# Late stages of a local-attention and feed-forward kernel: probabilities scaled in place in float32, split into two halves by one copy and one subtraction per two heads, with another table of scheduling numbers

## The chip, the cores and the metric

The kernel runs on one core of a Trainium2 chip. The metric is the device time of one execution in microseconds (us). The core has five engines that run side by side, each through a queue of its own in a fixed order: TensorE (PE, matrix products; PEld is its weight load), VectorE (DVE), ScalarE (ACT), GpSimd (POOL) and SyncE (SP, which here only issues DMAs). An engine that waits holds back everything behind it in its queue.

## The reference

For 4 batches of 768 positions with 8 heads of 64, every query sees the keys less than 16 positions away, and 24 block keys (the maxima of blocks of 32 keys, whose values are the blocks' means). The result of all heads, 3072 rows of 512, goes through two matrices with a SiLU between them.

```python
k_sum = k.reshape(B, H, nb, block, D).max(axis=3)
v_sum = v.reshape(B, H, nb, block, D).mean(axis=3)
scores_l = scale * np.matmul(q, k.transpose(0, 1, 3, 2))
...
scores_s = scale * np.einsum('bhsd,bhnd->bhsn', q, k_sum)
scores_s = scores_s + np.log(block)
...
a = np.exp(scores_all)
a = a / (np.sum(a, axis=-1, keepdims=True) + 1e-09)
...
h = x @ w_in
g = h * (1.0 / (1.0 + np.exp(-h)))
return (g @ w_out).astype(np.float32)
```

## The kernel before

**Tiles.** Attention runs over 24 tiles of 128 queries (s = 0 to 23, six for each batch b). Each query half of 64 sees 120 keys (64 + 32 local ones and 24 block keys), so that a head's scores are 128 x 120. The feed-forward part runs over 12 chunks of 256 rows (c = 0 to 11, two tiles each), and each chunk over 16 slices f of the 2048 inner columns.

**Number formats.** Attention of batch 0 and the whole of chunk 0 are computed in float32. From batch 1 on (the late stages of the title), queries, keys, probabilities and values are each split into a float16 part and the float16 rest of it, and a product is the sum of three float16 products. From chunk 1 on the feed-forward products are made in the same way, with weights that are split on the chip once their largest magnitude is known.

**One feed-forward step** (job_f): 12 matmuls of 256 columns into a bank (L818, float32: L815 and L837), tanh on ACT (L842), its product with the bank on DVE (L843), the float16 part on ACT (L845), the rest on DVE (L846), and 6 matmuls of 512 columns (L826, float32: L823) that add to two output banks. After the 16th step the output banks are scaled into a staging buffer (L871 on ACT, L872 on DVE) and written out (L873).

**One late attention tile:** scores on PE (job_scores, L591, 48 matmuls), then in job_a for each pair of heads: mask and row minimum of the negated scores on DVE (L627), exponential and row sum on ACT (L630), the inverse sums on DVE (L635, L636), the scaled probabilities in float16 (L670 by the helper `scaled`, on DVE, ACT or POOL: L645, L641, L643), and the rest of them, `e * sum - p`, on DVE (L674, two instructions per two heads). A DMA transposes the 128 x 512 tile of two heads and both parts (L677). Then 48 matmuls with the values (job_c, L709) and a copy with its split into x (job_x, L725 and L726). The values come by DMA, are scaled (L560, L561), copied to float16 (helper `copy`: L231 ACT, L233 POOL, L235 DVE) and their rest is taken (helper `less`: L238, on POOL or DVE). In tiles of batch 0 PE transposes the probabilities (L656) and multiplies them (L694).

**The weights:** 16 slices are loaded (L737), put right bit by bit (L755 and L751 on ACT, L753 and L757 on DVE), and their largest magnitude is taken (L758 on DVE). When all are there, a chain finds one scale: DVE L776, PE L781, DVE L785 to L790, PE L794, DVE L795 (it writes `ws`). Only then can the slices be split (L771 ACT or L772 DVE for the first part, L773 DVE for the rest), and L818 of chunk 1 can begin.

**Banks.** The score banks of all tiles from s = 4 on are 6 and 3 (L576); bank 3 is also an output bank of chunk 0, so its first scores wait until L871 has emptied it. Staging buffers for loads, outputs and values are a ring of three (`raw`).

**What sets the order.** All steps are handed to a planner (class Plan) with a cost for each engine that could do them, the keys that they read and write, and a priority. A sweep over a model of the machine picks the engine and the order; several rounds with priorities from a backward sweep follow. DVE and POOL steps that touch the port they share are never put side by side (`port`). Where PE would idle in the first stage, the planner puts filling matmuls (L325). The priorities come from the table TUNE, so that a change of a cost or of that table moves steps on all engines. Within an engine the order is then fixed in the program.

Of the kernel before, what the change touches and what calls it, by code (L numbers as in the profile page):

```python
# [16 lines left out]
ALU = mybir.AluOpType  # L17
# [5 lines left out]
P = 128  # L23
# [7 lines left out]
NKEY = HALF + BLK + NB  # L31
# [193 lines left out]
def local_attn_ffn(ctx: ExitStack, tc: tile.TileContext, qkT, qP, qF, kF, v, vR, vP, w, out):  # L225
# [383 lines left out]
    def job_a(m, prio):  # L609
# [28 lines left out]
        def scaled(e, out, j, i):  # L638
            by, src = su4[:, 2 * j + i:2 * j + i + 1], e_t[ns[j]][:, i, :]
            if e == "act":  # L640
                nc.scalar.activation(out=out, in_=src, func=AF.Copy, scale=by)  # L641
            elif e == "pool":
                nc.gpsimd.tensor_scalar(out=out, in0=src, scalar1=by, scalar2=0.0, op0=ALU.mult, op1=ALU.add)  # L643
            else:
                nc.vector.tensor_scalar(out=out, in0=src, scalar1=by, scalar2=None, op0=ALU.mult)  # L645
# [19 lines left out]
        for j, n in enumerate(ns):  # L665
            pk, et = (m + j) % NP, e_t[n]
            pt, (tt, ttk) = p_t[pk], tt_of(m + j)
            pkeys = [("p", pk, i) for i in range(2)]
            for i in range(2):
                plan.op({"dve": 235, "act": 296, "pool": 320}, lambda e, i=i, j=j, pt=pt: scaled(e, pt[:, i, :NKEY], j, i), r=[sum_key(j, i), ("e", n, i)], w=[pkeys[i]], prio=prio)  # L670

            def low(e, pt=pt, et=et, j=j):
                for i in range(2):
                    nc.vector.scalar_tensor_tensor(out=pt[:, i, P:P + NKEY], in0=et[:, i, :], scalar=su4[:, 2 * j + i:2 * j + i + 1], in1=pt[:, i, :NKEY], op0=ALU.mult, op1=ALU.subtract)  # L674

            plan.op({"dve": 510}, low, r=[sum_key(j, i) for i in range(2)] + [("e", n, i) for i in range(2)], w=pkeys, prio=prio)
            plan.op({"dma": 1250}, lambda e, tt=tt, pt=pt: nc.sync.dma_start_transpose(out=tt, in_=pt.rearrange("p a b -> p (a b)")), r=pkeys + ["third"], w=[ttk], prio=prio)  # L677

    def job_c(m, prio):
# [277 lines left out]
    plan.issue()  # L957


TUNE = dict(vd=145.25, ws=-1296.0, s0=-1306.0, wp=-955.25, wm=1695.25, km=296.75, w_dma=-551.75, w_dec=-1473.75, a0=-15.0, a1=-399.75, d1=7.75, span=34.25, post=1219.25, ffn2=350.75, jc0=150.5, jc1=208.75, jx0=-166.75, jx1=-108.0, vs=25.0, qk=66.0, k=57.5, v=2313.0, v0=-101.0, out=-36.75, first=771.75)  # L960


NUDGE = {}
# [58 lines left out]
```

## Time and profile before

| what | value |
|---|---|
| three timed runs, median (lowest to highest) | 599.84 us (599.81 to 600.15) |
| the profiled execution: its own time | 599.46 us |
| its span (first to last instruction) | 597.8 us |
| first matmul, last matmul start | 1.4 us, 593.8 us |
| ACT, share of the span | 62% |
| granted TensorE clock over the span | 1.00 |
| moved by DMA | 75.29 MB |

The span is what the views of the trace divide; 1.7 us of the execution lie outside it. In a timeline row stand the start and the length in us, the engine, the line, the operation, the tiles (out<-in), how many instructions were merged, and in brackets the idle time before it with what ended it. PE's rows are longer than its pace, since matmuls overlap; float32 matmuls appear as two instructions each.

### The profile page before, as it was taken

What the parts mean: (1) busy time and instruction counts of PE and PEld (TensorE: products, weight loads), DVE (VectorE), ACT (ScalarE), POOL (GpSimd) and SP (SyncE); (2) the same over time, 40 slices, a digit from 0 to 9 for tenths busy, and PEclk for the clock granted to TensorE, in tenths of its full rate; (3) what the DMA queues carried; (4) which work ended last, traced back from release to release, by engine and by line L of the source; (5) the groups of instructions that cost most, each with busy time, mean ns of one, the idle gap of its engine ahead of it and who ended that gap; (6) DMA issues with size and microseconds to landing.
All of it is one profiled execution on the core that took longest, in us unless ns stands there. A gap on an engine that the chain in (4) does not pass through costs nothing.

```text
span 597.8 us, 15304 instructions
## 1 busy us (share of the span) xinstructions
PE 588.6 (98%) x5848; PEld 399.7 (67%) x5848; DVE 440.1 (74%) x1338; ACT 372.2 (62%) x1014; POOL 108.6 (18%) x164
## 2 busy tenths in 40 slices
PE   8999999999999999999999999999999999999997
PEld 5666656676666666666666666666766766666664
DVE  6999979997886748979896555979898764333332
ACT  4998859777757756647675544756777554333332
POOL 3211201035421000043330020014241400000000
PEclk9999999999999999999999999999999999999999
DMA  8999532135765634543646530442734401000001
GB/s 334 410 420 412 174 123 98 27 87 152 153 128 172 157 90 128 90 133 97 123 129 174 166 89 36 120 122 62 169 93 106 111 2 36 36 1 2 35 1 37
DMA packets 60916, 75.29 MB, mean 126 GB/s; under 512 B 41914, under 2 KB 42170, under 8 KB 59050
## 3 DMA queue, kind: packets, MB, share of 16 engines
q1 hardware_dynamic: 60842, 74.31, 41.9%
q8 instruction: 46, 0.75, 0.5%
q14 instruction: 28, 0.23, 0.1%
HBM read 56.79 MB, written 6.29 MB: 106 GB/s over the span
## 4 chain that ended last, share of the span: by engine, by line
PE 82%; DVE 9%; DMA 4%; ACT 3%; issue 1%; SPq 1%; DVEq 0%; ACTq 0%
PE bank L826 37%; PE bank L818 37%; PE bank L709 3%; DVE wm L758 2%; PE bank L591 2%; DVE wr L757 2%; DMA raw<-in_qkT_dram 1%; DMA second<-in_qP_dram 1%; DVE e L627 1%; PE bank L694 1%; ACT wr L771 1%; PE bank L656 1%; DVE t L843 1%; PE bank L837 1%; DMA raw<-in_qF_dram 1%
## 5 line engine op out<-in xcount | busy, mean ns | idle before, releaser
L818 PE MATMUL bank<-x,wr 128*128 128x256 f16 x2112 | 258.1, 273 | 0.0
L818 PEld LDWEIGHTS <-wr 128*128 128x128 f16 x2112 | 205.6, 98 | 57.2 <-issue 0.6
L826 PE MATMUL bank<-wr,gh 128*128 128x512 f16 x702 | 209.1, 380 | 0.4 <-ACT gh L845 0.4
L843 DVE SCALAR_TENSOR_TENSOR t<-t,bank 128x256 f32<-128x256 f32 x192 | 80.1, 417 | 85.9 <-ACT t L842 85.0
L842 ACT ACTIVATE t<-bank,th 128x256 f32<-128x256 f32 x176 | 82.1, 467 | 92.7 <-PE bank L818 92.4
L826 PE MATMUL bank<-wr,gl 128*128 128x512 f16 x351 | 133.1, 379 | 0.1
L845 ACT ACTIVATE gh<-t 128x256 f16<-128x256 f32 x176 | 72.9, 414 | 72.3 <-DVE t L843 69.4
L846 DVE SCALAR_TENSOR_TENSOR gl<-t,gh 128x256 f16<-128x256 f32 x176 | 86.6, 493 | 40.4 <-ACT gh L845 40.0
L826 PEld LDWEIGHTS <-gh 128*128 128x128 f16 x702 | 65.9, 98 | 44.6 <-ACT gh L845 0.7
L630 ACT ACTIVATE e<-e,mx 128x120 f32<-128x120 f32 x192 | 73.2, 383 | 12.9 <-DVE mx L627 12.7
L826 PEld LDWEIGHTS <-gl 128*128 128x128 f16 x351 | 34.3, 98 | 43.7 <-DVE gl L846 3.0
L674 DVE SCALAR_TENSOR_TENSOR first<-e,sum,first 128x120 f16<-128x120 f32 x144 | 49.8, 394 | 0.3 <-POOL first L643 0.3
L643 POOL TENSOR_SCALAR first<-e,sum 128x120 f16<-128x120 f32 x52 | 22.0, 433 | 125.7 <-ACT gh L845 39.6
L627 DVE CUSTOM_DVE_ANT_0 e<-bank,masks,qsc 128x120 f32<-128x120 f32 x144 | 42.2, 336 | 2.8 <-PE bank L591 2.8
L630 ACT ACTIVATION_READ_ACCUMULATOR e<-e,mx 128x1 f32 x192 | 36.4, 190 | 0.0
L238 POOL TENSOR_TENSOR first<-raw,first 120x1024 f16<-120x1024 f32 x14 | 30.4, 2173 | 10.9 <-ACT first L231 5.4
L823 PE MATMUL bank<-wr,t 128*128 128x512 f32 x64 | 30.7, 599 | 0.0
L815 PE MATMUL bank<-x,wr 128*128 128x256 f32 x112 | 26.3, 379 | 0.0
L815 PEld LDWEIGHTS bank<-x,wr 128*128 128x128 f32 x112 | 21.0, 190 | 7.0 <-issue 4.1
L643 POOL TENSOR_SCALAR e<-e,sum 128x120 f32<-128x120 f32 x28 | 11.2, 412 | 71.4 <-DVE sum L636 61.8
L561 POOL TENSOR_SCALAR raw<-raw,vsc 120x1024 f32<-120x1024 f32 x10 | 11.7, 1167 | 55.5 <-PE bank L818 31.0
L773 DVE SCALAR_TENSOR_TENSOR wr<-wr,ws 128x1024 f16<-128x1024 f32 x16 | 20.2, 1274 | 0.1
(146 smaller groups left out, 598.1 us busy)
## 6 DMA issues: line engine op xcount, KB each, us to landing
wr<-in_w_dram SPq DMA_DIRECT2D x14, 1024.0 KB
raw<-in_qkT_dram SPq DMA_DIRECT2D x18, 576.0 KB
out_dram<-raw SPq DMA_DIRECT2D x23, 256.0 KB
raw<-in_kF_dram SPq DMA_DIRECT2D x12, 384.0 KB
raw<-in_qF_dram SPq DMA_DIRECT2D x9, 512.0 KB
raw<-in_vR_dram SPq DMA_DIRECT2D x12, 384.0 KB
raw<-in_v_dram SPq DMA_DIRECT2D x18, 208.0 KB
raw<-in_v_dram SPq DMA_DIRECT2D x18, 192.0 KB
```

What stands on the lines that cost most here:

```text
L627: plan.op({"dve": 262 if b else 206}, lambda e, i=i, j=j, et=et, mx=mx: nc.vector.tensor_tensor_reduce(out=et[:, i, :], in0=sc[j][:, i, :N ...
L630: plan.op({"act": 385}, lambda e, i=i, j=j, et=et, mx=mx: nc.scalar.activation(out=et[:, i, :], in_=et[:, i, :], func=AF.Exp, scale=-1.0, ...
L643: nc.gpsimd.tensor_scalar(out=out, in0=src, scalar1=by, scalar2=0.0, op0=ALU.mult, op1=ALU.add)
L674: nc.vector.scalar_tensor_tensor(out=pt[:, i, P:P + NKEY], in0=et[:, i, :], scalar=su4[:, 2 * j + i:2 * j + i + 1], in1=pt[:, i, :NKEY], o ...
L815: nc.tensor.matmul(out=h, lhsT=wi[:, ct * P:(ct + 1) * P], rhs=x0[:, ct, :], start=(ct == 0), stop=(ct == NCT - 1))
L818: nc.tensor.matmul(out=h, lhsT=wip[:, part, ct * P:(ct + 1) * P], rhs=x[:, ct, :], start=(ct == 0 and q == 0), stop=(ct == NCT - 1 and q = ...
L823: nc.tensor.matmul(out=bank[ob[u]], lhsT=t[:, u * P:u * P + P], rhs=wo, start=opens, stop=closes)
L826: nc.tensor.matmul(out=bank[ob[u]], lhsT=g[:, u * P:u * P + P], rhs=wop[:, part, :], start=(opens and q == 0), stop=(closes and q == 2))
L842: plan.op({"act": 264 if c == 0 else 360}, lambda e: nc.scalar.activation(out=t, in_=h, func=AF.Tanh, scale=0.5 if c == 0 else th[:, 0:1]) ...
L843: plan.op({"dve": 337}, lambda e: nc.vector.scalar_tensor_tensor(out=t, in0=t, scalar=1.0, in1=h, op0=ALU.add, op1=ALU.mult), r=bk(k), w=[ ...
L845: plan.op({"act": 311}, lambda e: nc.scalar.activation(out=gh, in_=t, func=AF.Copy, scale=SHRINK), r=[("t", j)], w=[("gh", n)], prio=post)
L846: plan.op({"dve": 343}, lambda e: nc.vector.scalar_tensor_tensor(out=gl, in0=t, scalar=SHRINK, in1=gh, op0=ALU.mult, op1=ALU.subtract), r= ...
```

## The change

For tiles of batches 1 to 3, job_a now scales the exponentials in place in float32 (the result goes to `e`, as it does for batch 0), then one copy makes the float16 part of two heads at once (2 x 120 columns, on DVE, ACT or POOL), and one subtraction of the same 240 columns makes the rest (on DVE or POOL). The subtraction reads the scaled float32 values, where L674 multiplied again. The table TUNE has other numbers throughout.

```diff
             for i in range(2):
-                plan.op({"dve": 235, "act": 296, "pool": 320}, lambda e, i=i, j=j, pt=pt: scaled(e, pt[:, i, :NKEY], j, i), r=[sum_key(j, i), ("e", n, i)], w=[pkeys[i]], prio=prio)
-
-            def low(e, pt=pt, et=et, j=j):
-                for i in range(2):
-                    nc.vector.scalar_tensor_tensor(out=pt[:, i, P:P + NKEY], in0=et[:, i, :], scalar=su4[:, 2 * j + i:2 * j + i + 1], in1=pt[:, i, :NKEY], op0=ALU.mult, op1=ALU.subtract)
-
-            plan.op({"dve": 510}, low, r=[sum_key(j, i) for i in range(2)] + [("e", n, i) for i in range(2)], w=pkeys, prio=prio)
+                plan.op({"dve": 160, "act": 296, "pool": 320}, lambda e, i=i, j=j, n=n: scaled(e, e_t[n][:, i, :], j, i), r=[sum_key(j, i)], w=[("e", n, i)], prio=prio)
+            ekeys = [("e", n, i) for i in range(2)]
+            hi, lo = pt[:, :, :NKEY], pt[:, :, P:P + NKEY]
+            plan.op({"dve": 193, "act": 282, "pool": 360}, lambda e, hi=hi, et=et: copy(e, hi, et), r=ekeys, w=pkeys, prio=prio)
+            plan.op({"dve": 320, "pool": 600}, lambda e, hi=hi, lo=lo, et=et: less(e, lo, et, hi), r=ekeys, w=pkeys, prio=prio)
...
-TUNE = dict(vd=145.25, ws=-1296.0, s0=-1306.0, wp=-955.25, wm=1695.25, km=296.75, w_dma=-551.75, w_dec=-1473.75, a0=-15.0, ...
+TUNE = dict(vd=150.75, ws=-1357.0, s0=-1615.75, wp=-777.5, wm=1870.5, km=248.5, w_dma=-556.5, w_dec=-1176.75, a0=5.25, ...
```

The instructions of the changed program, by engine, where the counts differ for this code (line numbers of before; below L676 the changed file's are 2 less):

| step | before | after |
|---|---|---|
| scaling, late tiles and batch 0 together: DVE L645 / ACT L641 / POOL L643 | 47 / 65 / 80 | 60 / 66 / 66 |
| copy of 240 columns: DVE / ACT / POOL | none | 17 / 35 / 20 |
| rest: L674 on DVE (120 columns) | 144 | none |
| rest: subtraction of 240 columns, DVE / POOL | none | 16 / 56 |
| filling matmuls L325 | 53 | 54 |

All other matmuls are the same in number and shape. Three pieces of the order follow; the number behind a tile's name only tells tiles apart.

DVE, where the scale of the weights is made (bank_184 is bank 6, raw_119 a staging buffer with a load of values, t and bank_178, bank_179 a step of chunk 0), before:

```order
L758 TENSOR_REDUCE wm<-wr 128x2
L776 TENSOR_REDUCE wx<-wm 128x2
L843 SCALAR_TENSOR_TENSOR t_167<-t_167,bank_179 128x256
L785 TENSOR_REDUCE wc<-bank_184 1x2
L786 TENSOR_SCALAR wc<-wc 1x2
L454 TENSOR_REDUCE am<-raw_119 128x1
L787 TENSOR_SCALAR wc<-wc 1x2
L452 TENSOR_REDUCE vm<-raw_119 128x24
```

The same place in the changed program:

```order
L756 TENSOR_REDUCE wm<-wr 128x2
L454 TENSOR_REDUCE am<-raw_119 128x1
L774 TENSOR_REDUCE wx<-wm 128x2
L452 TENSOR_REDUCE vm<-raw_119 128x24
L783 TENSOR_REDUCE wc<-bank_184 1x2
L841 SCALAR_TENSOR_TENSOR t_169<-t_169,bank_179 128x256
L784 TENSOR_SCALAR wc<-wc 1x2
L785 TENSOR_SCALAR wc<-wc 1x2
L786 TENSOR_SCALAR wc<-wc 1x2
L787 RECIPROCAL wc<-wc 1x2
```

The two reductions of a values load (L454, L452) stood inside the chain, behind its fourth step; now they stand ahead of L785 (now L783). On SP, the load of the last weight slice, which stood ahead of the first load of queries (L385), now stands behind it.

PE at the end of chunk 0 (bank_180 and bank_181 are the output banks 2 and 3), before:

```order
L781 MATMUL bank_184<-ident,wx 1x128 x2
L815 MATMUL bank_178<-x_164,wr 128x256 x4
L815 MATMUL bank_179<-x_164,wr 128x256 x4
L823 MATMUL bank_180<-wr,t_167 128x512
L794 MATMUL bank_184<-wc,ones 128x4
L823 MATMUL bank_181<-wr,t_167 128x512
L823 MATMUL bank_180<-wr,t_168 128x512
L823 MATMUL bank_180<-wr,t_169 128x512
L823 MATMUL bank_181<-wr,t_168 128x512
L823 MATMUL bank_181<-wr,t_169 128x512
```

And in the changed program:

```order
L813 MATMUL bank_179<-x_164,wr 128x256 x4
L779 MATMUL bank_184<-ident,wx 1x128 x2
L813 MATMUL bank_178<-x_164,wr 128x256 x4
L821 MATMUL bank_180<-wr,t_167 128x512
L821 MATMUL bank_181<-wr,t_167 128x512
L792 MATMUL bank_184<-wc,ones 128x4
L821 MATMUL bank_180<-wr,t_168 128x512
L821 MATMUL bank_181<-wr,t_168 128x512
L821 MATMUL bank_180<-wr,t_169 128x512
L821 MATMUL bank_181<-wr,t_169 128x512
```

L781 stands four L815 later, and L794 has one L823 more ahead of it and four instead of five behind it.

ACT at the same place (raw_118 is the staging buffer of chunk 0's output), before:

```order
L771 ACTIVATE wr<-wr,ws 128x2x512 x3
L871 ACTIVATE raw_118<-bank_180 128x512
L771 ACTIVATE wr<-wr,ws 128x2x512
L871 ACTIVATE raw_118<-bank_181 128x512
L771 ACTIVATE wr<-wr,ws 128x2x512
L842 ACTIVATE t_166<-bank_178,th_146 128x256
```

And in the changed program:

```order
L769 ACTIVATE wr<-wr,ws 128x2x512 x3
L869 ACTIVATE raw_118<-bank_180 128x512
L869 ACTIVATE raw_118<-bank_181 128x512
L769 ACTIVATE wr<-wr,ws 128x2x512
L840 ACTIVATE t_166<-bank_178,th_146 128x256
```

The emptying of bank 3 (bank_181) moved ahead of a split of weights, and one split fewer stands ahead of the first tanh of chunk 1. On DVE, four L773 instead of five stand ahead of the L843 that follows that tanh.

More of the change, by code (lines that the diff above doesn't have):

```diff
@@ L957, in local_attn_ffn @@
     plan.issue()
-TUNE = dict(vd=145.25, ws=-1296.0, s0=-1306.0, wp=-955.25, wm=1695.25, km=296.75, w_dma=-551.75, w_dec=-1473.75, a0=-15.0, a1=-399.75, d1=7.75, span=34.25, post=1219.25, ffn2=350.75, jc0=150.5, jc1=208.75, jx0=-166.75, jx1=-108.0, vs=25.0, qk=66.0, k=57.5, v=2313.0, v0=-101.0, out=-36.75, first=771.75)
+TUNE = dict(vd=150.75, ws=-1357.0, s0=-1615.75, wp=-777.5, wm=1870.5, km=248.5, w_dma=-556.5, w_dec=-1176.75, a0=5.25, a1=-404.5, d1=89.0, span=8.0, post=1362.5, ffn2=439.5, jc0=431.0, jc1=171.75, jx0=-87.5, jx1=-60.0, vs=-78.5, qk=157.0, k=69.25, v=2473.75, v0=-49.5, out=121.5, first=946.0)
 NUDGE = {}
```

## The prediction

> **What bounds the kernel.** I read the page's busy times first, then PE's busy time by stages, then the chain of waits, then what PE and its weight loads wait for.
>
> ```profile
> PE 588.6 (98%) x5848; PEld 399.7 (67%) x5848; DVE 440.1 (74%) x1338; ACT 372.2 (62%) x1014; POOL 108.6 (18%) x164
> ```
>
> The columns of the next view are PE, PEld, DVE, ACT and POOL busy (and instructions), the granted clock, the DMA share and GB/s.
>
> ```profile
> 0.00:30.00 30.00, 26.84 (x388) 18.92 (x389) 23.08 (x101) 20.37 (x59) 9.32 (x35) 1.00 0.95 373
> 30.00:75.00 45.00, 44.29 (x283) 30.85 (x282) 44.21 (x81) 39.12 (x83) 9.56 (x17) 1.00 0.85 335
> 75.00:105.00 30.00, 28.84 (x213) 18.71 (x212) 25.46 (x63) 23.12 (x55) 2.89 (x5) 1.00 0.32 106
> 105.00:420.00 315.00, 315.00 (x3364) 214.39 (x3362) 250.10 (x801) 205.08 (x586) 67.64 (x84) 1.00 0.45 116
> 420.00:445.00 25.00, 24.54 (x297) 16.60 (x296) 22.86 (x81) 18.06 (x63) 7.76 (x10) 1.00 0.54 126
> ```
>
> From 105 to 420 us PE is busy 315.00 of 315 us; what it lacks elsewhere is 3.16 + 0.71 + 1.16 + 0.46 = 5.5 us, nearly all of it ahead of 105 us. Busy is not yet pace, so two pieces of the chain follow.
>
> ```profile
> 98.72 1.31 PE bank L818 x12
> 588.91 4.53 PE bank L826 x21
> ```
>
> That is 109 ns for 256 columns and 216 ns for 512. The second piece lies at the end, where no attention is left; the first, in mid-work, keeps the same ratio per column. 2112 L818 and 1053 L826 at this pace make 457 us that no other engine can shorten. The late stages, where all rewritten instructions lie, are bound by PE, and DVE's load there is beside the path. What can move the time is PE's waits in the first 105 us, where the new table re-deals the order, and any new waits behind.
>
> **The rewritten steps.** Their prices come from these groups.
>
> ```profile
> L674 DVE SCALAR_TENSOR_TENSOR first<-e,sum,first 128x120 f16<-128x120 f32 x144 | 49.8, 394 | 0.3 <-POOL first L643 0.3
> L645 DVE TENSOR_SCALAR first<-e,sum 128x120 f16<-128x120 f32 x47 | 12.2, 292 | 0.2
> L643 POOL TENSOR_SCALAR first<-e,sum 128x120 f16<-128x120 f32 x52 | 22.0, 433 | 125.7 <-ACT gh L845 39.6 <-DVE sum L636 34.0 <-ACT t L842 14.2
> L235 DVE CAST first<-raw 120x1024 f16<-120x1024 f32 x4 | 2.8, 691 | 0.5 <-PE bank L709 0.3 <-DMA raw<-in_qF_dram 0.2
> L238 POOL TENSOR_TENSOR first<-raw,first 120x1024 f16<-120x1024 f32 x14 | 30.4, 2173 | 10.9 <-ACT first L231 5.4 <-DVE first L235 4.6
> L233 POOL TENSOR_SCALAR first<-raw 120x1024 f16<-120x1024 f32 x12 | 12.9, 1071 | 26.3 <-PE bank L709 19.5 <-ACT raw L560 6.5
> L231 ACT COPY third<-bank 120x256 f32<-120x256 f32 x15 | 4.9, 371 | 2.0 <-DVE third L235 1.1 <-PE bank L656 0.9
> ```
>
> DVE loses 144 L674 (49.8 us) and 47 L645 (12.2 us). It gains 60 scalings in place, not seen on DVE before: I bound one by zero and by L645's 292 ns. It gains 17 copies of 240 columns, between 240/1024 of 691 ns (0.16 us) and twice 292 ns, and 16 subtractions, between one and two L674 (0.39 to 0.79 us). That adds 9 to 40 us: DVE is relieved by 22 to 53 us. POOL loses 52 L643 into float16 (22.0 us) and gains 38 more in place at about the same 0.43 us (16 us), 20 copies between 0.25 us (240/1024 of 1071) and 0.87 us (two of 433), and 56 subtractions between 0.51 us (240/1024 of 2173) and 1.0 us. Its load rises by 28 to 67 us, from 18% to under a third of the span. ACT gains 35 copies near 0.37 us, 13 us. On the path all this counts **zero**, between the 0.46 us that PE lacks from 420 to 445 us (the most that there is to win) and the price of the second rival. The cover is PE's own 315 of 315 us, and the time that a pair's probabilities have after their transposition. The tightest tile I found:
>
> ```profile
> 427.37 3.82 SPq L677 DMA_TRANSPOSE third<-first  x3
> ...
> 432.26 0.95 PE L709 MATMUL bank<-third,first 120*64 120x64 f16 x48
> ```
>
> The first of these three transposes is that tile's last; with 1.2 us each it ends near 428.6 us, 3.7 us ahead of its L709. The chain of two heads grows from scaling and L674 to scaling, copy and subtraction, at most 0.87 + 1.0 - 2 x 0.39 = 1.1 us. Gone, that cover would cost PE a wait at each of 18 tiles; at 1.1 us it is not gone.
>
> **The moved steps** set the sum. Chunk 0 ends like this:
>
> ```profile
> 74.84 3.60 PE L823 MATMUL bank<-wr,t 128*128 128x512 f32 x8
> ...
> 76.10 1.22 DVE L758 TENSOR_REDUCE wm<-wr 128x2 f32<-128x1024 f32 x1
> ...
> 78.27 0.38 PE L781 MATMUL bank<-ident,wx 128*1 128x128 f32 x2
> ...
> 78.49 3.62 PE L815 MATMUL bank<-x,wr 128*128 128x256 f32 x16
> 78.69 0.41 DVE L785 TENSOR_REDUCE wc<-bank 1x2 f32<-1x256 f32 x1 [0.59 <-PE bank L781]
> 79.14 0.16 DVE L786 TENSOR_SCALAR wc<-wc 1x2 f32<-1x2 f32 x1
> ...
> 80.54 0.95 DVE L454 TENSOR_REDUCE am<-raw 128x1 f32<-128x768 f32 x1 [1.25 <-DMA raw<-in_vR_dram]
> ...
> 81.95 1.02 PE L823 MATMUL bank<-wr,t 128*128 128x512 f32 x2
> ...
> 82.92 0.15 DVE L790 SCALAR_TENSOR_TENSOR wc<-wc 1x1 f32<-1x1 f32 x1
> ...
> 83.12 0.38 PE L794 MATMUL bank<-wc,ones 1*128 1x4 f32 x2
> ...
> 83.73 1.15 ACT L771 ACTIVATE wr<-wr,ws 128x1024 f16<-128x1024 f32 x1 [1.20 <-DVE ws L795]
> ...
> 86.25 6.31 DVE L773 SCALAR_TENSOR_TENSOR wr<-wr,ws 128x1024 f16<-128x1024 f32 x5
> ...
> 87.83 1.47 PE L818 MATMUL bank<-x,wr 128*128 128x256 f16 x12
> ...
> 88.46 0.57 ACT L871 ACTIVATE raw<-bank 128x512 f32<-128x512 f32 x1
> 88.94 1.14 ACT L771 ACTIVATE wr<-wr,ws 128x1024 f16<-128x1024 f32 x1
> ...
> 89.98 0.58 ACT L871 ACTIVATE raw<-bank 128x512 f32<-128x512 f32 x1
> ...
> 90.61 0.31 PE L594 MATMUL bank<-first,second 64*64 64x96 f32 x3 [1.01 <-ACT raw L871]
> ```
>
> DVE stands idle 1.25 us inside the scale's chain, for a load that the chain doesn't need. An L823 instruction takes 0.43 us, twice an L826 (eight took 3.60 us with the last one's tail), so PE is free at 81.95 + 0.86 = 82.81 and waits 0.31 us for L790. In the new order L454 and L452 come ahead, so L790 follows L785 after one L843 (0.4 us) and four steps near 0.2 us. But L781 stands eight float32 L815 later (half of the 3.62 us that sixteen took, less the tail: 1.73 us): at 80.0, which puts L790's end near 82.3. PE reaches L794 one L823 pair later, at 82.81 + 0.86 = 83.67. The chain no longer binds, and the 0.31 us go; L794 itself stands 0.55 us later.
>
> From L794 the path runs over ACT: 5.3 us to the first L871, 7.5 us to L594, with one L771 between the two L871. The new order takes that L771 out: 88.94 to 89.98, 1.04 us less. So L594 comes at 83.67 + 7.49 - 1.04 = 90.12 instead of 90.61: **-0.49 us**. PE has a shorter tail of L823 and will wait a little for the first L773 and still for L871; that is in this number.
>
> All that PE gains ahead of 82 us comes through, since L794 is then reached by PE. What there is to gain:
>
> ```profile
> 66.77 0.45 PE L694 MATMUL bank<-third,wr 120*64 120x64 f32 x8 [0.71 <-ACT third L231]
> ```
>
> There ACT did an L725 and an L755 ahead of the copies that PE waits for. The new order has the L755 behind them, but all four copies on ACT, and less work on PE meanwhile: I take -0.4 us of 0.71. In the first 30 us PE lacks 3.16 us, of which this wait can't go:
>
> ```profile
> PE bank L325 <- POOL ident masks.py:199: 1.4, 1, 1.4
> ```
>
> Batch 0's scalings, transposes and x copies are dealt anew among ACT, DVE and POOL, and one filling matmul is added (0.11 us). I take -0.2 us net, out of -1.8 us (all the rest that PE lacks there) to +1.4 us (two more waits like the 0.71 us above). I choose near zero because no row speaks for either end. Together **-0.6 us** (-2.5 to +1.4).
>
> Behind L594, one L771 (1.14 us) less stands ahead of the first L842, and one L773 (6.31/5 = 1.26 us) less ahead of its L843. PE's weight loads wait for the rests L846 in all of the program:
>
> ```profile
> PEld L826 <- DVE gl L846: 3.0, 7, 0.5
> ```
>
> Seven times, 0.5 us at most. I take **-0.2 us** for the first of them (0 to -0.5).
>
> **The sum** against the profiled execution: 599.46 - 0.49 - 0.6 - 0.2 + 0 = 598.2 us. That execution lies 0.38 us under the median of the timed runs (599.84), so the forecast for a median is **598.5 us**, 0.22% less.
>
> **Rivals.** *First, the gains cancel.* The re-dealt start costs what the rest brings. For it: PE's first 30 us hang on short chains over four engines, and the only stretch that I could work out in full gives 0.5 us. Against it: the waits at 66 and 90 us have causes that the new order removes. With +0.7 us at the start in place of -0.6: 599.84 - 0.49 - 0.2 + 0.7 = 599.8 us. Here belongs also that the change doesn't relieve DVE at all (that scaling in place costs as much as before): with PE full, it is not seen in the time.
>
> *Second, it is slower: POOL's subtractions hold DVE.* In this trace DVE's L488, 850 ns in the mean, took three times that beside a subtraction on POOL:
>
> ```profile
> 412.97 2.18 POOL L238 TENSOR_TENSOR first<-raw,first 120x1024 f16<-120x1024 f32 x1
> ...
> 413.08 2.62 DVE L488 SCALAR_TENSOR_TENSOR second<-raw,qsc,second 128x512 f16<-128x512 f32 x1
> ```
>
> The 56 new ones can each hold an L846 for 0.51 to 1.0 us, and PE's L826 waits for L846. Against it: the 18 L238 of before are there already, longer ones, and L826 waited for L846 only 3.0 us in all. If one in four cost PE 0.3 us, 14 x 0.3 = 4.2 us come on top: 602.7 us. It decides from 2.5 us on, some eight such hits of 0.3 us. The Trainium skill speaks for this rival (SBUF — State Buffer, "Who interferes with whom"): a DVE instruction with two inputs in SBUF and a GpSimd instruction that reads SBUF exclude each other for the whole instruction. This trace agrees, with 2.62 us for L488 beside 2.18 us on POOL.
>
> **Chances.** The forecast, faster: 0.50. The first rival: 0.37. The second: 0.13. This kernel's measurement can tell 0.2% from no change, so faster means under 598.6 us and slower over 601.0 us. The range goes from 596.3 us (the start's low end, 1.9 us further, and a part of what is to win at the rests and from 420 to 445 us) to 601.2 us (the high end of the start with a few hits of the second rival); the second rival's full price is left out.
>
> **What would show it.** L594 behind the first L818 of chunk 1 waits under 0.6 us and starts near 89.5 us; L794 starts without a wait; no wait of 0.7 us near 66 us. DVE's busy time falls to 387 to 418 us and POOL's rises to 137 to 176 us, while PE stays at 315 of 315 us from 105 to 420 us. I am wrong if PE lacks more than a microsecond behind 105 us, with L846 or L709 as the one waited for, or if the first L837 step starts later than before.

## The result, and the profile after

The change is slower: 606.20 us in the median of seven runs (602.80 to 607.36), the kernel before beside it 599.84 (599.40 to 602.60). The ratio is 1.0089, with a 95% interval of 1.0064 to 1.0113 (it is not the quotient of the two medians, 1.0106). The median lies outside the forecast range (596.3 to 601.2 us), on the side that was given a chance of 0.13. The profiled execution took 603.99 us with a span of 602.2 us, 4.4 us more than the span before. Its busy times, and the stages in the columns used for the profile before:

```profile
PE 590.3 (98%) x5849; PEld 400.7 (67%) x5849; DVE 420.0 (70%) x1240; ACT 383.1 (64%) x1053; POOL 146.2 (24%) x223
```

```profile
0.00:30.00 30.00, 27.21 (x389) 19.25 (x390) 22.61 (x106) 21.64 (x74) 10.18 (x37) 1.00 0.96 375
30.00:75.00 45.00, 44.20 (x282) 30.54 (x281) 42.07 (x70) 39.02 (x76) 7.36 (x13) 1.00 0.85 338
75.00:105.00 30.00, 28.96 (x209) 18.23 (x208) 24.93 (x59) 21.52 (x50) 3.03 (x5) 1.00 0.30 99
105.00:420.00 315.00, 311.34 (x3289) 212.15 (x3288) 237.58 (x724) 212.85 (x610) 97.02 (x128) 0.99 0.48 116
420.00:445.00 25.00, 25.00 (x343) 17.16 (x341) 20.90 (x82) 20.32 (x66) 13.65 (x24) 1.00 0.67 140
```

VectorE is relieved (440.1 to 420.0 us) and GpSimd loaded (108.6 to 146.2 us), as the change says. Ahead of 105 us TensorE lacks 4.63 us, 0.40 us less than before; from 420 to 445 us its 0.46 us are gone. The loss is in the stage that was full before: from 105 to 420 us it now lacks 3.66 us (315 - 311.34), and the clock column fell to 0.99. The waits of TensorE over the whole program name one place above all:

```profile
PE bank L707 <- DVE x L724: 2.8, 1, 2.8
PE bank L325 <- POOL ident masks.py:199: 1.4, 1, 1.4
PE bank L824 <- DVE gl L844: 0.7, 1, 0.7
...
PE bank L594 <- ACT raw L869: 0.4, 1, 0.4
...
PE bank L692 <- ACT t L840: 0.4, 1, 0.4
PE bank L816 <- DVE wr L771: 0.2, 1, 0.2
```

(L707 is L709 of before, L724 is L726, L824 is L826, L844 is L846, and so on by two.) The timeline of the changed kernel at this one wait of 2.8 us:

```profile
175.33 1.31 DVE L645 TENSOR_SCALAR e<-e,sum 128x120 f32<-128x120 f32 x2
...
175.53 1.04 POOL L233 TENSOR_SCALAR first<-raw 120x1024 f16<-120x1024 f32 x1
...
175.86 0.58 ACT L723 ACTIVATE x<-bank 128x512 f16<-128x512 f32 x1
...
176.65 2.12 POOL L238 TENSOR_TENSOR first<-raw,first 120x1024 f16<-120x1024 f32 x1
...
176.89 2.03 DVE L235 CAST first<-e 128x240 f16<-128x240 f32 x1
...
178.84 0.60 DVE L635 TENSOR_SCALAR sum<-sum 128x4 f32<-128x4 f32 x1
179.35 0.40 DVE L238 TENSOR_TENSOR first<-e,first 128x240 f16<-128x240 f32 x1
179.67 0.68 DVE L724 SCALAR_TENSOR_TENSOR x<-bank,x 128x512 f16<-128x512 f32 x1
...
180.40 1.25 PE L707 MATMUL bank<-third,first 120*64 120x64 f16 x48 [2.76 <-DVE x L724]
```

L724 is the last reader of the bank that this L707 needs. Its other input (L723, ScalarE) is there at 176.44 us (175.86 + 0.58), but L724 stands in VectorE's queue behind the new copy L235. That copy began 0.24 us after GpSimd's subtraction of a value tile, an old step of 1024 columns, and ended 0.15 us after it: 2.03 us. The clock, by stretches of 10 us (TensorE busy, granted clock, DMA share, GB/s):

```profile
170.00:180.00 10.00, 7.64 (x97) 1.00 0.39 43
180.00:190.00 10.00, 9.60 (x93) 0.83 0.46 84
```

The sum closes: TensorE lacks 8.29 us up to 445 us (4.63 + 3.66 + 0.00) where it lacked 5.49 before, 2.80 us more, and 10 us at 0.83 are another 1.7 us: 4.5 us against the 4.4 us by which the span grew.

**The theories.** First: one collision at a place without slack, as read above. Second: the planner's prices for the new steps are too low, so that its schedule runs late everywhere. Third: the new table's order costs it, whatever the instructions (a deal, below, is one assignment of all steps to engines and places). Fourth: the new instructions cost it wherever they stand.

### The profile page after: what moved, and what is told of

The parts are those of the page before. It is cut to its first block, busy times and chain, and to the rows that moved or that the text cites. A ratio compares the mean times of both kernels' runs of the same rounds, so it can differ in the third digit from the quotient of the medians.

```text
span 602.2 us, 15253 instructions
## 1 busy us (share of the span) xinstructions
PE 590.3 (98%) x5849; PEld 400.7 (67%) x5849; DVE 420.0 (70%) x1240; ACT 383.1 (64%) x1053; POOL 146.2 (24%) x223
## 4 chain that ended last, share of the span: by engine, by line
PE 77%; DVE 9%; ACT 6%; DMA 3%; issue 2%; POOL 1%; SPq 1%; POOLq 0%; DVEq 0%; ACTq 0%
PE bank L824 35%; PE bank L816 34%; PE bank L707 3%; DVE wm L756 2%; PE bank L591 2%; DMA raw<-in_qkT_dram 1%; ACT wr L769 1%; DVE e L627 1%; DVE wr L755 1%; DMA wr<-in_w_dram 1%; ACT wr L753 1%; DMA second<-in_qP_dram 1%; DVE t L841 1%; ACT wr L749 1%; ACT t L840 1%
## 5 line engine op out<-in xcount | busy, mean ns | idle before, releaser
L816 PE MATMUL bank<-x,wr 128*128 128x256 f16 x2112 | 258.8, 273 | 0.2 <-DVE wr L771 0.2
L816 PEld LDWEIGHTS <-wr 128*128 128x128 f16 x2112 | 205.8, 98 | 58.7 <-issue 1.1
L824 PE MATMUL bank<-wr,gh 128*128 128x512 f16 x702 | 210.0, 381 | 0.0
L841 DVE SCALAR_TENSOR_TENSOR t<-t,bank 128x256 f32<-128x256 f32 x192 | 80.2, 418 | 104.7 <-ACT t L840 104.0
L824 PE MATMUL bank<-wr,gl 128*128 128x512 f16 x351 | 133.6, 380 | 0.7 <-DVE gl L844 0.7
L844 DVE SCALAR_TENSOR_TENSOR gl<-t,gh 128x256 f16<-128x256 f32 x176 | 84.0, 479 | 41.4 <-ACT gh L843 40.9
L843 ACT ACTIVATE gh<-t 128x256 f16<-128x256 f32 x176 | 72.6, 413 | 59.3 <-DVE t L841 53.6
L824 PEld LDWEIGHTS <-gh 128*128 128x128 f16 x702 | 66.2, 98 | 44.3 <-ACT x L723 0.3
L824 PEld LDWEIGHTS <-gl 128*128 128x128 f16 x351 | 34.4, 98 | 43.0 <-DVE gl L844 1.5
L643 POOL TENSOR_SCALAR e<-e,sum 128x120 f32<-128x120 f32 x66 | 28.7, 443 | 111.6 <-DVE sum L636 54.7
L238 POOL TENSOR_TENSOR first<-e,first 128x240 f16<-128x240 f32 x56 | 38.1, 690 | 53.5 <-ACT first L231 50.9
L627 DVE CUSTOM_DVE_ANT_0 e<-bank,masks,qsc 128x120 f32<-128x120 f32 x144 | 41.6, 336 | 0.4 <-PE bank L591 0.4
L233 POOL TENSOR_SCALAR second<-ks 128x384 f16<-128x384 f16 x10 | 6.0, 600 | 99.6 <-PE bank L591 84.3
L813 PE MATMUL bank<-x,wr 128*128 128x256 f32 x112 | 26.8, 383 | 0.7 <-DVE t L841 0.7
L813 PEld LDWEIGHTS bank<-x,wr 128*128 128x128 f32 x112 | 20.8, 190 | 8.2 <-issue 3.1
L641 ACT ACTIVATE e<-e,sum 128x120 f32<-128x120 f32 x66 | 23.2, 384 | 1.7 <-DVE sum L636 1.7
L771 DVE SCALAR_TENSOR_TENSOR wr<-wr,ws 128x1024 f16<-128x1024 f32 x16 | 20.4, 1283 | 1.2 <-ACT wr L769 1.1
```

What stands on the lines that cost most here:

```text
L238: eng[e].tensor_tensor(out=out, in0=in0, in1=in1, op=ALU.subtract)
L627: plan.op({"dve": 262 if b else 206}, lambda e, i=i, j=j, et=et, mx=mx: nc.vector.tensor_tensor_reduce(out=et[:, i, :], in0=sc[j][:, i, :N ...
L813: nc.tensor.matmul(out=h, lhsT=wi[:, ct * P:(ct + 1) * P], rhs=x0[:, ct, :], start=(ct == 0), stop=(ct == NCT - 1))
L816: nc.tensor.matmul(out=h, lhsT=wip[:, part, ct * P:(ct + 1) * P], rhs=x[:, ct, :], start=(ct == 0 and q == 0), stop=(ct == NCT - 1 and q = ...
L824: nc.tensor.matmul(out=bank[ob[u]], lhsT=g[:, u * P:u * P + P], rhs=wop[:, part, :], start=(opens and q == 0), stop=(closes and q == 2))
L841: plan.op({"dve": 337}, lambda e: nc.vector.scalar_tensor_tensor(out=t, in0=t, scalar=1.0, in1=h, op0=ALU.add, op1=ALU.mult), r=bk(k), w=[ ...
```

## The experiments

All times are medians beside runs of the kernel before on the same chip. There were four groups of runs; the medians of before in them are 599.69 us (again, later_sub, both oldorder), 599.96 (repaired, split_sub, both with a swapped table), 599.78 (repaired2, before_fixed, fixed_newpool) and 600.06 (three, nine, bank3), so kernels of different groups are best compared by their ratios. "Lacks" is what TensorE lacks of the 315 us from 105 to 420 us in that kernel's one profile, which need not be of a middling run: that of later_sub is its fastest of 12. The two kernels with a swapped table have four runs each.

| kernel | median (lowest to highest), us | ratio to before, 95% interval | lacks, us |
|---|---|---|---|
| again (the change unaltered) | 603.73 (601.39 to 606.09) | 1.0055 (1.0031 to 1.0079) | 5.45 |
| later_sub (one exchange) | 601.03 (599.57 to 604.26) | 1.0007 (0.9988 to 1.0026) | 1.53 |
| split_sub | 603.16 (601.87 to 604.12) | 1.0056 (1.0035 to 1.0077) | 3.05 |
| oldorder_newdve | 601.01 (600.30 to 604.70) | 1.0022 (1.0001 to 1.0042) | 0.74 |
| oldorder_newpool | 600.36 (598.85 to 601.63) | 0.9997 (0.9978 to 1.0016) | 0.00 |
| newcode_oldtable | 604.79 (603.52 to 612.43) | 1.0102 (1.0052 to 1.0153) | 2.41 |
| oldcode_newtable | 606.11 (604.25 to 607.17) | 1.0094 (1.0066 to 1.0122) | 3.93 |
| three (exchanges) | 603.75 (602.05 to 605.60) | 1.0057 (1.0038 to 1.0076) | 4.44 |
| repaired (six) | 602.23 (599.46 to 604.95) | 1.0040 (1.0022 to 1.0057) | 2.93 |
| repaired2 (nine) | 601.26 (600.25 to 604.70) | 1.0029 (1.0013 to 1.0045) | 1.68 |
| nine | 601.13 (598.65 to 606.83) | 1.0024 (1.0001 to 1.0046) | 1.56 |
| before_fixed | 599.87 (598.64 to 602.45) | 0.9999 (0.9985 to 1.0014) | 0.24 |
| fixed_newpool | 599.67 (598.81 to 601.98) | 0.9998 (0.9984 to 1.0012) | 0.00 |
| bank3 | 599.48 (598.85 to 604.47) | 0.9998 (0.9981 to 1.0016) | 0.26 |

### Is it chance? The change once more

> The changed kernel unaltered, for a second profile and times beside those of the next three. Theory 1 (one collision at a place without slack: at 176.9 us VectorE's copy L235 takes 2.03 us beside GpSimd's 2.12 us subtraction L238 of a value tile, L724 behind it comes late, L707 waits 2.76 us for it, and TensorE's clock is then granted at half for about 3 us): this wait stands in the second profile too, at 2 to 3 us, and the time is 603 to 607. If the cause lies in one execution's chance (a late DMA, the clock alone): the wait is under 1 us or stands elsewhere, at about the same time of 603 to 607.

The second profile has the same collision, and a longer wait:

```profile
176.88 2.12 POOL L238 TENSOR_TENSOR first<-raw,first 120x1024 f16<-120x1024 f32 x1
177.11 2.03 DVE L235 CAST first<-e 128x240 f16<-128x240 f32 x1
...
179.90 0.68 DVE L724 SCALAR_TENSOR_TENSOR x<-bank,x 128x512 f16<-128x512 f32 x1
...
180.63 0.95 PE L707 MATMUL bank<-third,first 120*64 120x64 f16 x48 [3.29 <-DVE x L724]
```

```profile
170.00:180.00 10.00, 7.33 (x95) 1.00 0.39 47
180.00:190.00 10.00, 9.37 (x145) 1.00 0.48 86
```

The wait is no chance. The lower clock is not part of it: after 3.29 us without work the clock stayed at 1.00. This execution lost the same 4.4 us of span in another way, with a second collision that the first profile did not have:

```profile
298.47 2.44 POOL L238 TENSOR_TENSOR first<-raw,first 120x1024 f16<-120x1024 f32 x1
298.85 2.75 DVE L491 SCALAR_TENSOR_TENSOR second<-raw,qsc,second 128x640 f16<-128x640 f32 x1
...
301.52 0.41 DVE L841 SCALAR_TENSOR_TENSOR t<-t,bank 128x256 f32<-128x256 f32 x1
...
304.57 0.75 DVE L844 SCALAR_TENSOR_TENSOR gl<-t,gh 128x256 f16<-128x256 f32 x2
305.04 0.39 PE L824 MATMUL bank<-wr,gl 128*128 128x512 f16 x1 [1.20 <-DVE gl L844]
```

### The collision taken away

On GpSimd the value subtraction changes places with the subtraction of probabilities behind it; nothing else moves on any engine.

```diff
 L233 TENSOR_SCALAR first<-raw_118 120x1024
-L238 TENSOR_TENSOR first<-raw_118,first 120x1024
-L238 TENSOR_TENSOR first<-e_159,first 128x2x120
+L238 TENSOR_TENSOR first<-e_159,first 128x2x120
+L238 TENSOR_TENSOR first<-raw_118,first 120x1024
```

> The changed kernel with one pair of GpSimd's instructions exchanged: the subtraction L238 of a value tile that stood beside the copy at 176.9 us goes behind the subtraction of probabilities that followed it. Theory 1: the copy takes about 0.3 us, L724 follows some 2 us sooner, L707 waits under 1 us there and the granted clock stays at 1.0 in 180 to 190: 2 to 4.5 us less than the changed kernel. Theory 2 (the plan's prices for the new steps are too low, so that the whole schedule runs late) and theory 3 (the new table's denser order loses everywhere): within 1 us of the changed kernel. Against theory 1 too: the moved subtraction now holds the next VectorE instructions (L635, L238) instead, and the wait stays above 2 us.

The timeline of this kernel at the same place, and its stage from 105 to 420 us:

```profile
175.25 0.58 ACT L723 ACTIVATE x<-bank 128x512 f16<-128x512 f32 x1
...
176.27 0.27 DVE L235 CAST first<-e 128x240 f16<-128x240 f32 x1
...
176.91 0.68 DVE L724 SCALAR_TENSOR_TENSOR x<-bank,x 128x512 f16<-128x512 f32 x1
...
177.16 0.64 POOL L238 TENSOR_TENSOR first<-e,first 128x240 f16<-128x240 f32 x1 [1.21 <-ACT first L231]
...
177.64 0.95 PE L707 MATMUL bank<-third,first 120*64 120x64 f16 x48 [0.65 <-DVE x L724]
...
177.76 2.31 POOL L238 TENSOR_TENSOR first<-raw,first 120x1024 f16<-120x1024 f32 x1
178.00 0.41 DVE L841 SCALAR_TENSOR_TENSOR t<-t,bank 128x256 f32<-128x256 f32 x1
```

```profile
105.00:420.00 315.00, 313.47 (x3352) 213.43 (x3350) 237.89 (x734) 217.01 (x617) 99.70 (x131) 1.00 0.47 118
```

The copy takes 0.27 us, L724 follows the end of L723 by 1.08 us instead of 3.23, and the wait is 0.65 us. The median falls by 2.7 us against the unaltered change beside it (603.73 to 601.03), and the ratio to before is 1.0007 where it was 1.0055: in this order, this one place held most of the loss. The first theory's numbers came out; the second and third gave no reason for them. Of the 1.53 us still lacking, 0.72 us is one wait at 109 us (L824 for L844, which stands behind two L771 of 1.3 us on VectorE) and 0.65 us is the one above.

### How long is VectorE held?

Here each of the 14 value subtractions on GpSimd is given as four of 256 columns.

```diff
-        eng[e].tensor_tensor(out=out, in0=in0, in1=in1, op=ALU.subtract)
+        for c in pieces(e, out): eng[e].tensor_tensor(out=out[c], in0=in0[c], in1=in1[c], op=ALU.subtract)
```

(`pieces` gives the four parts on GpSimd for a value tile, and otherwise the whole.)

> The changed kernel in its own order, with each of GpSimd's 14 value subtractions of 1024 columns given as four of 256 columns. Theory 1, in the form that VectorE's copy waits for the whole of a GpSimd instruction that has begun: at 176.9 us the copy waits at most about 0.6 us instead of 1.76, L707 waits under 2 us, and the long VectorE steps beside such subtractions elsewhere (L491, L645) shorten too; 1 to 3 us less than the changed kernel, 601 to 603. If GpSimd keeps VectorE out between its instructions as well: the copy ends only behind the fourth, wait and time as in the changed kernel or slightly worse, 603.5 to 605.

```profile
177.62 2.83 POOL L238 TENSOR_TENSOR first<-raw,first 120x256 f16<-120x256 f32 x4
177.86 0.57 DVE L235 CAST first<-e 128x240 f16<-128x240 f32 x1
...
179.95 0.95 PE L707 MATMUL bank<-third,first 120*64 120x64 f16 x48 [1.60 <-DVE x L724]
```

The copy now waits for one piece, 0.57 us instead of 2.03, so it is the GpSimd instruction under way that holds it, to its end and no longer. The wait is 1.60 us, as the first theory said, and the profiled execution took 601.87 us. But it was the fastest of seven: the median of 603.16 us is no better than the change's. The four pieces take 2.83 us where one took 2.12, and L635 (0.63 us) and L844 (0.92 us) behind were held as well. The median, just above the 601 to 603 us expected, stays unexplained by this one profile.

### The instructions or the order?

Two kernels keep the order of before and put the new instructions where the old ones stood. The second line with `less` is that of oldorder_newpool:

```diff
-  ... scaled(e, pt[:, i, :NKEY], j, i) ...
+  ... scaled(e, e_t[n][:, i, :], j, i) ...
-  for i in range(2): nc.vector.scalar_tensor_tensor(out=pt[:, i, P:P + NKEY], in0=et[:, i, :], ...)
+  copy("dve", pt[:, :, :NKEY], et)
+  less("dve", pt[:, :, P:P + NKEY], et, pt[:, :, :NKEY])
+  less("pool", pt[:, :, P:P + NKEY], et, pt[:, :, :NKEY])
```

> The order of before, with the new instructions put in place of the old ones: probabilities scaled in place on the engine that scaled them before, and VectorE's two L674 of a pair replaced by one copy and one subtraction of 240 columns, both on VectorE. Theories 1 and 3 (the order and its places decide): within 1 us of before, VectorE some 5 to 9 us less busy. Theory 4 (the instructions themselves cost it, wherever they stand): 3 to 6 us above before. Theory 2: within 1 us of before, since nothing here is planned by the prices.

> The order of before, probabilities scaled in place, the two L674 of a pair replaced by a copy on VectorE and all 72 subtractions of 240 columns on GpSimd at the place where L674 stood. Theory 1: GpSimd's 72 times 0.64 us hold VectorE for moments at many places; where the order of before has slack this costs nothing, so within 2 us of before, and where it costs, the waits are for a VectorE instruction that ran beside one of them. The rival of the prediction (GpSimd's subtractions delay L846 generally): 2 to 4 us above before, with many waits of L826 of some 0.3 us. Theory 3: within 1 us of before.

With all 72 subtractions on GpSimd TensorE is full again:

```profile
105.00:420.00 315.00, 315.00 (x3365) 214.56 (x3363) 242.34 (x755) 206.23 (x588) 99.75 (x134) 1.00 0.44 116
```

The ratio of 0.9997 excludes the fourth theory for the order of before, and there the prediction's second rival with it: 72 subtractions, more than the change's 56, cost nothing that can be told in an order with slack. With everything on VectorE it is 1.0022, at the edge of what can be told; the 0.74 us it lacks do not explain more. One expectation of this run failed: VectorE was to be 5 to 9 us less busy and is 4 us busier (444.3 us, before 440.1), since the 72 copies and 72 subtractions take 23.1 + 34.1 = 57.2 us where the L674 took 49.8. The new steps relieve VectorE only where they go to another engine.

The other two swap the table of numbers between the kernels, one line each:

```diff
-TUNE = dict(vd=150.75, ws=-1357.0, ...
+TUNE = dict(vd=145.25, ws=-1296.0, ...
```

> The code of the change with the table of before: the planner deals the new steps with the old numbers. The instructions are the new ones, the order is neither of the two. Theory 1: the time depends on which VectorE steps this order sets beside long GpSimd instructions without slack behind them, so that it may fall anywhere from 598 to 607, and each loss over 0.5 us behind 105 us is found at one place with a held VectorE instruction or a queue ahead of it. Theory 2: above 602, spread over many small waits. Theory 3 (the new table alone): within 1.5 us of before.

> The code of before with the table of the change: the old instructions, dealt by the new numbers. Theory 1: anywhere from 598 to 607, with the losses at single places as above, since the old steps are held by the 2.2 us GpSimd subtractions too. Theory 2: within 1.5 us of before, since the old prices stand. Theory 3: 603 to 606, as the change.

Both lose about 1%. In newcode_oldtable 1.98 of the 2.41 us lacking are two waits at 146 and 148 us (the longest, 1.5 us, is L591 for L627, which stands behind other steps in VectorE's queue). The old code with the new table has no new instruction in it and loses what the change loses (1.0094, and 1.0089): the second theory, which gave it no loss, falls. Its longest wait, 1.96 us (L826 for L846, at 301.92 us), follows a hold of the same kind, on an old instruction:

```profile
294.30 3.40 DVE L674 SCALAR_TENSOR_TENSOR first<-e,sum,first 128x120 f16<-128x120 f32 x2
...
295.44 2.13 POOL L238 TENSOR_TENSOR first<-raw,first 120x1024 f16<-120x1024 f32 x1
```

Behind these two L674, which take 0.60 us at 281.73 us in the same kernel, stands L843, and ScalarE waited 3.47 us for it at the head of its queue. That this hold made the later wait is read from the profile; no run takes it away. The third theory is right in that a new deal costs, but the old table costs the new code the same, so it is no property of the new numbers: three deals, the change's own among them, came out about 1% slower than the order of before. Why that one is better, no run shows.

### Can the new order be mended?

repaired adds five exchanges to later_sub, repaired2 three more. The three that matter below, on VectorE:

```diff
 L645 TENSOR_SCALAR e_158<-e_158,sum_150 128x120 x2
 L841 SCALAR_TENSOR_TENSOR t_166<-t_166,bank_179 128x256
+L724 SCALAR_TENSOR_TENSOR x_165<-bank_185,x_165 128x4x128
 L235 CAST first<-e_158 128x2x120
...
-L771 SCALAR_TENSOR_TENSOR wr<-wr,ws 128x2x512 x2
-L844 SCALAR_TENSOR_TENSOR gl_175<-t_167,gh_171 128x256
+L771 SCALAR_TENSOR_TENSOR wr<-wr,ws 128x2x512
+L844 SCALAR_TENSOR_TENSOR gl_175<-t_167,gh_171 128x256
+L771 SCALAR_TENSOR_TENSOR wr<-wr,ws 128x2x512
...
+L841 SCALAR_TENSOR_TENSOR t_167<-t_167,bank_178 128x256
 L488 SCALAR_TENSOR_TENSOR second<-raw_118,qsc_132,second 128x512
 L491 SCALAR_TENSOR_TENSOR second<-raw_118,qsc_132,second 128x4x160
-L841 SCALAR_TENSOR_TENSOR t_167<-t_167,bank_178 128x256
```

> The changed kernel with six exchanges in the order, each for a wait read from the profiles: the value subtraction behind the subtraction of probabilities as before; L724 ahead of the copy L235 at 176 us; L844 ahead of one L771 at 107 us; L844 ahead of L454 at 130 us; L840 ahead of the copy of v on ScalarE at 66 us; TensorE's L792 one matmul earlier at 83 us. If these waits are what the new table costs (theory 1, and single places throughout): 2.0 to 3.0 us less than with the first exchange alone, about 597 to 598.5, so faster than before by 0.2 to 0.4%, with TensorE busy for over 314.5 of the 315 us from 105 to 420. If theories 2 or 3 hold, the waits turn up at other places, and it stays at 600 to 601.

> The changed kernel with the six exchanges of the run before and three more, at the places where that run's profile still lost time: L841 ahead of L488 and L491, which wait for a load, near 297 us; L844 ahead of L366, which waits for a load, near 201 us; L409 ahead of one L771 near 118 us. If the losses are single places (theory 1 in its wider form: whatever holds VectorE's queue, a GpSimd instruction or a load at its head, costs only where L841 or L844 stand behind it without slack): 1.5 to 2.8 us less than with six exchanges, 599.5 to 600.8. If the new order is short of slack nearly everywhere, so that other places take over: within 0.7 us of it, about 602, with new waits of L824 on L844 over 0.7 us behind 105 us.

> The changed kernel with three exchanges: the value subtraction behind the subtraction of probabilities (later_sub), L724 ahead of the copy at 176 us and L844 ahead of one L771 at 107 us, and none of those in the first 105 us. If the six exchanges came out worse than the first alone because TensorE reached 200 and 300 us sooner, where the loads at the head of VectorE's queue were not there yet: this one lies between, 601 to 602, with a wait of L824 near 200 or 300 us. If the waits are independent single places: 1.0 to 1.5 us less than with the first alone, 599.5 to 600.

> The changed kernel with nine exchanges, as in the earlier run with nine, except that L366 goes behind L844 at 197 us rather than L844 ahead of it, so that L844 reads the gh that L843 has just written. The earlier run computed one L844 from the gh of the chunk before, which spares it the wait for L843. If that did not matter: 600.5 to 601.5 as there. If it did: 0.3 to 0.8 us more, with L824 waiting for L844 near 203 us.

In repaired2 one L844 computes from the gh (the float16 part that L843 writes) of the step before, since L843 stands behind it, as the expectation of nine says. In nine, where L844 reads the right gh, the wait foretold for that case came (L824 for L844, 0.71 us at 204.62 us), but the two times agree within their intervals, so what repaired2 spares is too small to tell. The expectations for repaired and three were wrong, and repaired2 lies between its two. The waits mended behind 105 us went (the one near 66 us, L692's, stayed at 0.36 to 0.47 us in all kernels with that exchange, now put down to ScalarE's copy of v), but others came: L824 waited for L844 1.7 us near 300 us in repaired and in three, at the place of the collision in the second profile of the change. In both the first exchange and the second together moved the value subtraction onto an L844, here in three:

```profile
178.78 2.29 POOL L238 TENSOR_TENSOR first<-raw,first 120x1024 f16<-120x1024 f32 x1
179.01 2.34 DVE L844 SCALAR_TENSOR_TENSOR gl<-t,gh 128x256 f16<-128x256 f32 x1
```

With nine exchanges the ratio is 1.0024, still not below later_sub. So the losses are at single places, but the new order has several such places with little slack, and which of them strike changed with each set of exchanges and between two profiles of the same kernel. Three, which has later_sub's exchange in it, came out at 1.0057 and later_sub at 1.0007; the profile of three shows new waits (the 1.7 us above and six of 0.3 to 0.6 us), and why they arise is not settled.

### The prediction's first terms by themselves

before_fixed makes four exchanges in the kernel before, fixed_newpool the same four with the new instructions of oldorder_newpool. In both, the L846 that goes ahead of two L674 also stands ahead of its L845, so it computes from the gh of the step before and does not wait for its own: their times are those of kernels that leave this wait out.

> The kernel before, with its own instructions and table, and only four exchanges: the second eviction L871 ahead of one L771 at 89 us, which frees bank 3 for L594 (the prediction's first term by itself); L755 behind the copies of third on ScalarE at 65 us (the wait of 0.71 us that the prediction counted to the start); L843 ahead of L490, which waits for a load, at 429 us, and L846 ahead of two L674 at 436 us (the prediction's third term). If each term is worth what the prediction said where nothing else moves: 1.3 to 2.4 us less than before, 597.5 to 598.5. If the waits move on (L818 waits for L773's chunk instead, as it does in the changed kernel): within 0.7 us of before.

> The same four exchanges in the order of before, with the new instructions in place of the old ones: scaling in place, a copy on VectorE and all 72 subtractions of 240 columns on GpSimd. Since these instructions in the order of before came out within the uncertainty of before, the same time as the run with the four exchanges alone, within 1 us, is expected by theory 1; if GpSimd's subtractions meet VectorE more often now that the order is tighter at its start, 1 to 3 us above it.

bank3 makes the exchange at 89 us alone, with L842 ahead too:

```diff
 L871 ACTIVATE raw_118<-bank_180 128x512
-L771 ACTIVATE wr<-wr,ws 128x2x512
 L871 ACTIVATE raw_118<-bank_181 128x512
-L771 ACTIVATE wr<-wr,ws 128x2x512
 L842 ACTIVATE t_166<-bank_178,th_146 128x256
-L771 ACTIVATE wr<-wr,ws 128x2x512 x2
+L771 ACTIVATE wr<-wr,ws 128x2x512 x4
```

> The kernel before with one exchange alone: at 89 to 92 us ScalarE's second eviction L871 and L842 go ahead of the two L771 that stand between and behind them. In the run with four exchanges L594's wait of 1.01 us went, but L826 then waited 0.8 us for gh (L845), since L842 stood behind both L771. If the prediction's first term can be had where L842 goes ahead too: the stretch from 75 to 105 us has TensorE busy for about 29.7 of 30 us (28.84 before), 0.7 to 1.1 us less than before. If the two L771, 1 us later, hold a chunk of weights that L818 waits for: the stretch stays below 29.2 and the time within 0.4 us of before.

All three are at 0.9998 or 0.9999 of before. The timeline of bank3, and one row of its waits:

```profile
87.93 5.00 DVE L773 SCALAR_TENSOR_TENSOR wr<-wr,ws 128x1024 f16<-128x1024 f32 x4
...
89.60 0.65 PE L594 MATMUL bank<-first,second 64*64 64x96 f32 x5
...
92.84 0.41 DVE L843 SCALAR_TENSOR_TENSOR t<-t,bank 128x256 f32<-128x256 f32 x1
```

```profile
PE bank L826 <- ACT gh L845: 1.2, 2, 0.9
```

L594 no longer waits, and TensorE is busy for 28.84 of 30 us from 75 to 105 us, exactly as before: behind it L826 now waits up to 0.9 us for L845, which follows L843, and L843 stands behind five L773 in VectorE's queue (the row shows the last four). With ScalarE's order mended, VectorE's is the limit there. The exchange at 65 us in before_fixed missed its wait too: L694 still waited 0.9 us and went on at 67.84 us, put down to ScalarE's copies of third, which had ended at 67.10; the copy that came last was VectorE's, begun at 67.66 us behind L726.

## Why the prediction was wrong, step by step

- **"On the path all this counts zero ... The cover is PE's own 315 of 315 us"** is the step that failed. For the instructions it holds (oldorder_newpool: 315.00 us, ratio 0.9997). For the change it does not, since the table deals all late steps anew. The prediction named "any new waits behind" as something that can move the time, and then gave them no term of their own. The cover was read from the order of before, and only for the probabilities' way from transposition to L709. The loss came by another way: L724, which empties L707's bank, behind a copy in VectorE's queue. In place of zero stand 3.66 us and a lower clock in one execution, 5.45 us in the other.
- **The second rival** had the mechanism, GpSimd holding VectorE, but laid it to the 56 new subtractions and some hits of 0.3 us on L846. It was the old value subtractions of 2.1 to 2.4 us, one or two hits of 1.2 to 3.3 us, and L724 first. Its 602.7 us was too low, and the time fell on its side by other instructions than those it priced.
- **-0.49 us for bank 3** failed too. From L794 to L594 the new order took 6.45 us (84.64 to 91.09), just what the prediction added up (7.49 - 1.04), and L594's wait fell from 1.01 to 0.42 us. But L794 (now L792) came at 84.64 us and not at 83.67, so L594 came later than before, L816 waited 0.24 us for L771, and TensorE gained only 0.12 us from 75 to 105 us. bank3 shows that the wait is given back behind it even when it is taken away alone: the step left out L773's row on VectorE, which ends near 92.6 us before and near 92.9 us in both the change and bank3.
- **-0.6 us for the start** was right in its larger part: the wait of 0.71 us became 0.38 (forecast -0.4), and the first 30 us gained 0.37 (forecast -0.2); L813's waits for L841 took some back. In all, 0.40 us came of the 1.09 us forecast ahead of 105 us, in the second profile too.
- **-0.2 us for the rests** did not show: the weight loads' waits for L844 fell from 3.0 to 1.5 us in all, but one of them is now 1.2 us, behind two L771, and TensorE waited 0.75 us there, at 109.83 us. The 0.46 us from 420 to 445 us, which the prediction counted zero, went.
- **The prices** (changed kernel's groups; mean ns of one behind the busy time) were within their bounds but one:

```profile
L238 POOL TENSOR_TENSOR first<-e,first 128x240 f16<-128x240 f32 x56 | 38.1, 690 | 53.5 <-ACT first L231 50.9 <-DVE first L235 1.1
...
L645 DVE TENSOR_SCALAR e<-e,sum 128x120 f32<-128x120 f32 x60 | 19.3, 354 | 0.3
...
L235 DVE CAST first<-e 128x240 f16<-128x240 f32 x17 | 7.1, 418 | 0.0
```

  Scaling in place was bounded by 292 ns and took 354, often beside GpSimd's work. The rewritten steps on VectorE took 19.3 + 7.1 + 7.2 = 33.6 us, inside the 9 to 40 forecast. VectorE's 420.0 us still lie just above the 387 to 418 forecast, since other steps grew: the 52 L635 went from 8.1 to 12.3 us, and four more evictions went to VectorE (5.0 to 7.9 us). GpSimd's 146.2 us lie in their forecast.
- The test named for being wrong was more than a microsecond lacking behind 105 us, with L846 or L709 as the one waited for. The amount came, but the row is L709 (now L707) waiting for L726 (now L724); the wait for L846 (now L844) was 0.75 us.

## What to carry to other kernels

Where a change comes with a new deal of the order, a full engine in the old profile is no cover by itself: read the cover again for every step whose lateness stops that engine, above all for the last reader of a bank that the next product needs. A planner that keeps two engines off a shared port in its model gives no wait that keeps them off it on the chip, so a long GpSimd instruction must not stand near a short VectorE step with no slack behind it. And before an early wait is counted as a gain, look for the queue that ends at the same time behind it.

## What the hardware showed

VectorE's copies from SBUF and its steps with two inputs in SBUF, begun beside a GpSimd subtraction, do not end before that has ended, whatever their own size: a copy of 0.27 us took 2.03, an L844 of 0.41 us took 2.34, an L491 of 0.87 us took 2.75, beside subtractions of 2.1 to 2.4 us, and in pieces the hold shrank to 0.57 us. L841, which reads a bank, took its usual 0.41 us inside a subtraction of 2.31 us. The Trainium skill (SBUF — State Buffer, "Who interferes with whom") says so: whoever issues first keeps the shared pair of ports for the whole instruction and the other blocks fully, and it counts copies in a two-port mode and operations with two inputs in SBUF among those concerned. These runs agree.

The clock was not expected to move: 0.83 over 10 us after a wait of 2.76 us in one execution, and 1.00 after a wait of 3.29 us in another. Cut at its edges, the lower clock is 0.50 for 3.41 us:

```profile
177.36:180.78 3.42, 0.66 (x27) 0.49 (x27) 3.42 (x6) 0.71 (x3) 2.05 (x2) 1.00 0.00 0
180.78:184.19 3.41, 3.41 (x42) 1.69 (x37) 2.10 (x5) 2.25 (x4) 0.89 (x1) 0.50 0.77 83
```

The Trainium skill (TensorE: Matmul & The Clock Gate, "What's actually happening") has the clock halve after an idle window of about 3.4 us whose windows run free. The traces agree, if a window counts as idle with a little work in it. Each trace's record of the clock begins at one such edge: at 6.70 us in this execution, 51 steps of 3.413 us ahead of 180.78, so the wait fell almost whole into one window, with 0.66 us of work. In the second profile it begins at 5.19 us, and the same steps put an edge at 179.27 us, which cuts the wait of 3.29 us in two, with 1.47 and 2.05 us of work on its sides. Shorter waits of 1.96 us (oldcode_newtable, at 301.92 us) and 1.48 us (newcode_oldtable, at 147.88 us) did halve the clock for 3.41 us; the windows ahead held 1.45 and 1.43 us of work. Cut this way, in all the profiles of this case every window with 1.45 us of work or less was followed by the lower clock, and none with more. So not the length of a wait decides, but how little work it leaves in one window, and where the edges fall is chance.

The lower clock is part of the price in the timed runs: the mean clock was 0.997 or less, as one such stretch makes it, in 5 of the 7 and 4 of the 10 timed runs of the change (606.2 and 605.1 us in the mean, the others 603.8 and 602.9), in 4 of the 35 of before beside again, and in none of the 12 of later_sub.
